# Spectral layer and GeGLU block on one core: the place of the filter sums, of the last n1 transform and of the fourth turn

## The chip, the cores and the metric

The kernel runs on one core of one Trainium2 chip. The core has a matrix engine (TensorE, in the profile PE for its matmuls and PEld for its weight loads), a vector engine (VectorE, DVE), a scalar engine (ScalarE, ACT), a general engine (GpSimd, POOL) and a queue engine (SyncE, SP), each with an instruction stream of its own. They are ordered among one another by semaphores only. Matmuls write to PSUM, which has eight banks; everything else lies in SBUF. The metric is the device time in microseconds (us). Before the change it is 502.81 us, the median of 8 runs (502.54 to 502.91).

## The reference

The input x has 2048 tokens of 576 values in bfloat16. Two sublayers are computed, each behind a layer norm:

```python
def _A_ref(x, w_r, w_i):
    B, S, D = x.shape
    X = rfft2(x.astype(float32), axes=(-2, -1))
    X = X * (w_r + 1j * w_i)
    return irfft2(X, s=(S, D), axes=(-2, -1)).astype(bfloat16)

def _B_ref(x, w_gate, w_up, w_down):
    return (gelu(x @ w_gate) * (x @ w_up)) @ w_down

h  = x + _A_ref(layernorm(x), w_r, w_i)
h2 = h + _B_ref(layernorm(h), w_gate, w_up, w_down)
```

The filter w_r + i w_i has 2048 x 289 values, w_gate and w_up are 576 x 4608, w_down is 4608 x 576.

## The kernel before

The kernel is written as one list of operations in program order. Each operation names its engine, the data it reads and the data it writes. From this list the kernel derives the waits: an operation waits for those before it, on any engine, whose data it needs or whose buffer it takes over. On PE the program order alone is relied on; on DVE, ACT and POOL a dependence inside the same engine is a wait as well. Each engine works off its own operations in the order of the list, so where an operation stands in the list settles what it queues behind.

Tokens are numbered s = 16 n1 + n2, with n1 on the 128 partitions; there are 16 token tiles, one for each n2.

**Layer norm and first transform** (to about 20 us). The statistics of the tiles are taken in five groups. Each group's reciprocal deviation scales the table of the n1 transform (ATS, line 472 on DVE for the first two groups and the last, line 467 on POOL for the third and fourth), and matmuls with x as weights give U, which DVE and ACT copy out of PSUM.

**Spectral stage** (about 20 to 53 us). The frequencies form 16 groups, worked through in the order 1 to 15, 0; in what follows group i is the i-th in this order. Each group goes through these steps:

- `st_D`: six matmuls (line 600), the transform over the 576 values, even and odd halves in two banks; ACT copies the even half (line 603).
- `st_U`: DVE adds the halves (A, line 610) and subtracts them (S, line 613).
- `st_B`: six matmuls (line 626), the rest of the n1 transform; ACT copies the result (YS, line 629).
- `st_T`: DVE multiplies by the filter in two products (T0, T1, line 635). One of them uses a negated copy of w_i, which POOL writes for each group (line 674).
- `st_Z`: DVE sums the two products (Z, line 640).
- `st_V`: six matmuls (line 654), the first part of the inverse n1 transform; ACT copies the result into V (line 665), for the last group DVE and ACT do so in three parts (lines 660 and 662).

One loop (line 676) runs these in a software pipeline: turn i issues `st_D` and `st_U` of group i, `st_B` and `st_T` of group i - 2, and `st_V` of group i - 4. The sum `st_Z` of group i - 3 is issued by `st_U` of group i, between its add and its subtract. The last groups differ: the sum of group 13 follows directly on its products, the last group's products and sums are cut into columns 0 to 127 and the rest, and the sum of group 14 stands behind the first of these products.

POOL's 16 negations wait for the halves of w_i that they use and for the last scaled table of the first transform, `("ATS", NT - 1)`, written by DVE. The loads of the filter are issued on SP's queue. On POOL's queue stand, behind the negations, the loads of the gate weights: those of the first two blocks directly, those of the last two where the filter's buffer comes free, after the last product.

**Inverse stage** (about 53 to 77 us). For each of the 16 tiles c, `st_I(c)` runs six matmuls (line 723), the inverse transform over the values, into two banks given by `islot`; ACT copies them into GS (line 732). `st_N(c)` runs four matmuls (line 762), the last part of the inverse n1 transform, into banks 4 to 7, and DVE adds the result to x (line 765). In program order `st_N(c - 1)` follows `st_I(c)`. The first block of four tiles is normalised on the way (`norm`, DVE and POOL) and turned by `turn_pe`: five matmuls with the unit matrix (line 807) into two banks of the pair used by `st_I`, which ACT copies into HT0 (line 809). `TURN` gives the steps after which the four turns are issued, 8, 10, 12 and 14; `islot` skips a bank pair behind each.

**Gate, up and down** (from about 75 us). Four blocks of 512 tokens. `gu` issues the gate and up matmuls (line 861), two at a time on 64 rows each, with a lag of six matmuls between the halves: `gu(0)` issues the first six of the first half alone. Behind them, still in `gu(0)`, stands `st_N` of the last tile, 15. ACT applies the gelu (line 873), DVE multiplies (line 874). Then the down matmuls (line 884) follow with the final add and the store.

```python
for i in range(NG + 4):
    if i < NG:
        st_D(i); st_U(i)
    ...
    if 2 <= i < NG + 2:
        st_B(i - 2)
    if 2 <= i <= NG:
        st_T(i - 2, 0); st_T(i - 2, 1)
    ...
    if i >= 4:
        st_V(i - 4)
```

Of the kernel before, what the change touches and what calls it, by code (L numbers as in the profile page):

```python
# [7 lines left out]
ALU = mybir.AluOpType  # L8

S, D, K2 = 2048, 576, 289  # L10
KW = 290
# [284 lines left out]
def _build(nc, A_x, A_w_r, A_w_i, B_w_gate, B_w_up, B_w_down, out):  # L296
# [76 lines left out]
    def banks(b, n, w):  # L373
        return PS[:, b * 512:(b + n) * 512].rearrange("p (a c) -> p a c", a=n)[:, :, 0:w]
# [215 lines left out]
    def dbank(i):  # L590
        return 6 if i == 2 else 2 * ((i if i < 2 else i - 3) % 2)

    def st_D(i):
# [7 lines left out]
                                                                        start=(dt == 0), stop=(dt == 2)),  # L601
                     r=uk[us] + ["FT"], w=[("PS", b)])
        P.op(ACT, lambda a, sl=sl, b0=b0: a.activation(ES[:, sl, :], bank(b0, 0, 128, 0, 2 * HK), ACTF.Copy), r=[("PS", b0)], w=[("E", sl)])


    def st_U(i):
        sl, b0, s3 = i % 2, dbank(i), i % 3
        e2 = ES[:, sl, :].rearrange("p (a b) -> p a b", a=2)
        o2 = bank(b0 + 1, 0, 128, 0, 2 * HK).rearrange("p (a b) -> p a b", a=2)
        P.op(DVE, lambda v, e2=e2, o2=o2, s3=s3: v.tensor_tensor(CUS[:, s3, :, 0:HK], e2, o2, op=ALU.add), r=[("E", sl), ("PS", b0 + 1)], w=[("CU", s3)])  # L610
        if i >= 3:
            st_Z(i - 3)
        P.op(DVE, lambda v, e2=e2, o2=o2, s3=s3: v.tensor_tensor(CUS[:, s3, :, K2 - 1:HK - 1:-1], e2[:, :, 0:HK - 1], o2[:, :, 0:HK - 1], op=ALU.subtract),  # L613
             r=[("E", sl), ("PS", b0 + 1)], w=[("SU", s3)])

# [14 lines left out]


    def st_T(i, t_, q0=0, q1=KW, hs=(0, 1)):
        g, sl = GORD[i], i % 2
        w_ = (slice(1, None, -1), slice(2, 0, -1))[t_]
        P.op(DVE, lambda v: v.tensor_tensor(TP[:, sl, t_, :, q0:q1], YS[:, sl, :, q0:q1], WS[:, g, w_, q0:q1], op=ALU.mult),  # L635
             r=[("Y", sl), ("Wn", i), "Yz", "Zz"] + wkeys[0 if 1 <= g < 9 else 1], w=[("T", sl, t_, h) for h in hs])

    def st_Z(i, q0=0, q1=KW, hs=(0, 1)):
        sl, z3 = i % 2, i % 3
        P.op(DVE, lambda v: v.tensor_tensor(ZS[:, z3, :, q0:q1], TP[:, sl, :, 0, q0:q1], TP[:, sl, :, 1, q0:q1], op=ALU.add),  # L640
             r=[("T", sl, t_, h) for t_ in range(2) for h in hs], w=[("Z", z3, h) for h in hs])


    VBANKS = {NG - 4: (0, 0, 1), NG - 2: (2, 2, 3), LAST: (0, 1, 4)}
# [27 lines left out]
    P.alias(["J0", "J1", "ZD"] + [(n_, c) for n_ in ("ATB", "ATS") for c in range(NT)], ["Vfree"])  # L672
    for i in range(NG):
        P.op(POOL, lambda v, g=GORD[i]: v.tensor_scalar(WS[:, g, 0, :], WS[:, g, 2, :], -1.0, None, op0=ALU.mult),  # L674
             r=[k for k in wkeys[0 if 1 <= GORD[i] < 9 else 1] if k[2] == 1] + ["Wz", ("ATS", NT - 1)], w=[("Wn", i)])
    for i in range(NG + 4):
        if i < NG:
            st_D(i)
            st_U(i)
        if i == NG:  # L680
            st_Z(NG - 3)
        if 2 <= i < NG + 2:
            st_B(i - 2)
        if 2 <= i <= NG:
            st_T(i - 2, 0)
            st_T(i - 2, 1)
        if i == NG + 1:
            st_T(LAST, 0, 0, 128, (0,))
            st_Z(LAST - 1)
            st_T(LAST, 1, 0, 128, (0,))  # L690
            st_T(LAST, 0, 128, KW, (1,))
            st_Z(LAST, 0, 128, (0,))
            st_T(LAST, 1, 128, KW, (1,))
            st_Z(LAST, 128, KW, (1,))
        if i == NG + 3:
            idle_ft(3, 5)
        if i >= 4:
            st_V(i - 4)
# [14 lines left out]
    vkeys = vk[0] + vk[1] + vk[2]  # L713


    TURN = (8, 10, 12, 14)

    def islot(c):
        return (c + sum(c > t for t in TURN)) % 2
# [36 lines left out]
    def st_N(c):  # L756
        sl = c % 2
        for h in range(2):
            b = 4 + 2 * sl + h
            for i in range(2):  # L760
                rhs = GS[:, sl, i, 288:0:-1] if h else GS[:, sl, i, 0:288]
                P.op(PE, lambda t, b=b, h=h, i=i, c=c, rhs=rhs: t.matmul(bank(b, 0, 128, 0, 288), IT[:, h * i, c, :], rhs, start=(i == 0), stop=(i == 1)),  # L762
                     r=[("G", sl, i), "IT"], w=[("PS", b)])
# [37 lines left out]
    def turn_pe(c):  # L801
        hs = c % 4
        t0, t1 = 128 * c, 128 * c + 128
        b0 = 2 * ((TURN[c] + 1 + c) % 2)
        for k in range(5):
            b, o = b0 + k // 4, 128 * (k % 4)
            P.op(PE, lambda t, b=b, o=o, k=k, hs=hs: t.matmul(bank(b, 0, 128, o, o + 128), HN[:, hs, 128 * k:128 * k + 128], IDT[:, :], start=True, stop=True),  # L807
                 r=[("HN", hs, 0), ("HN", hs, 1), "IDT"], w=[("PS", b)])
        P.op(ACT, lambda a, t0=t0, t1=t1, b0=b0: a.activation(HT0[:, 0:5, t0:t1], PS[:, b0 * 512:b0 * 512 + 640].rearrange("p (k e) -> p k e", k=5), ACTF.Copy),
             r=[("PS", b0), ("PS", b0 + 1)], w=[("HT", 0, c, 0)])  # L810

    st_I01()
    for c in range(1, NT):
        if c >= 2:
            st_I(c)
        st_N(c - 1)
        if 2 <= c < 6:
            square(c - 2, OS[:, c % 2, :], ("OS", c % 2, 0))
        if c == 5:
            ln2_a(0)  # L820
        if c == 6:
            ln2_b(0)
            ln2_c(0)
            norm(0, DVE)
            norm(1, POOL)
        if c == 7:
            norm(2, DVE)
            norm(3, POOL)
        if c in TURN:
            turn_pe(TURN.index(c))  # L830

    P.alias(ukeys + [(n_, a) for n_ in ("CU", "SU") for a in range(3)], [("WD", j) for j in range(9)])
    for j in range(9):
# [14 lines left out]
    def gu(n):  # L848
        for s_ in range(9 * (n - 1) + LAG, 9 * n + LAG):
            for half in range(2):  # L850
                m, j = divmod(s_ - LAG * half, 9)
                if not 0 <= m < 144:
                    continue
                tb, f = m // 36, m % 36
                o, wt = (ASEQ, BSEQ)[half][j]
                kt = 4 if wt == 8 else wt % 4
                h0 = 64 * half
                HT = HTS[tb % 2]
                b = 2 * (m % 3) + o
                aft = [half_done[m, o]] if half and (j == 0 or j == 4) else []  # L860
                op = P.op(PE, lambda t, h0=h0, kt=kt, wt=wt, f=f, b=b, HT=HT, s=(half == 0 and j in (0, 5)), e=(half == 1 and j in (3, 8)): t.matmul(  # L861
                    bank(b), WGU[h0:h0 + 64, f // 9, wt, 128 * (f % 9):128 * (f % 9) + 128], HT[h0:h0 + 64, kt, :], start=s, stop=e),
                    r=[("HT", tb % 2, i, k) for i in range(4) for k in range(5)] + [("WG", f // 9, i) for i in range(4)],
                    w=[("PS", b)], after=aft)
# [80 lines left out]
```

## Time and profile before

| | |
|---|---|
| median of 8 runs | 502.81 us (502.54 to 502.91) |
| the profiled execution's own time | 502.74 us |
| its span, first to last instruction | 500.9 us |
| mean granted TensorE clock | 0.997 |
| PE busy (matmuls) | 492.6 us, 98% of the span |
| DVE busy | 182.4 us, 36% |
| ACT busy | 158.4 us, 32% |
| POOL busy | 39.8 us, 8% |
| gate/up matmuls on the chain that ended last | 56% of the span |
| down matmuls on that chain | 28% |
| DVE on that chain | 7% |

The profile is one execution. The span leaves out what lies around the first and last instruction, 1.84 us here. "Busy" is the time in which an engine works on instructions, overlapping ones counted once; PE's matmuls are pipelined and their ends are modelled. The chain of waits goes back from the last instruction to whatever released it, and so on to the start. In rows of the timeline the first number is the start in us, the second the length in us of the instruction or, with x2 and the like, of several merged ones; the tiles stand as output <- inputs. "L640" is line 640 of the kernel.

### The profile page before, as it was taken

The numbers are of one execution on the slowest core, as the hardware profiler recorded it, in microseconds if no ns is written. First come the engines' busy times: TensorE is split into PE (matmuls) and PEld (weight loads), VectorE is DVE, ScalarE is ACT, GpSimd is POOL, SyncE is SP. The second block draws the span as 40 slices with busy tenths as digits, with TensorE's granted clock in tenths as the row PEclk, the third lists the DMA queues.
The fourth block names the chain that finished last, engine by engine and source line by source line (L and its number), as shares of the span: only waits on it lengthen the run. The fifth ranks groups of instructions, "written<-read, shape, count | busy, mean of one in ns | idle before, by whom it ended". The sixth has DMA issues, their size and how long they took to land.

```text
span 500.9 us, 9971 instructions
## 1 busy us (share of the span) xinstructions
PE 492.6 (98%) x4318; PEld 298.8 (60%) x4319; DVE 182.4 (36%) x391; ACT 158.4 (32%) x296; POOL 39.8 (8%) x49
## 2 busy tenths in 40 slices
PE   7999999999999999999999999999999999999998
PEld 2787774444457764444477744444677544444775
DVE  6899663344421114433311034433201233333111
ACT  7888776653220012323300023232100123233000
POOL 3654290000000000000000000000000000000000
PEclk9899999999999999999999999999999999999999
DMA  8769998001100000100000001100000000000000
GB/s 284 166 202 313 326 295 313 2 7 25 26 1 19 18 13 20 22 14 1 2 13 12 19 18 22 23 1 1 1 18 19 13 1 1 1 3 1 12 19 19
DMA packets 25948, 28.64 MB, mean 57 GB/s; under 512 B 11568, under 2 KB 19888, under 8 KB 25776
## 3 DMA queue, kind: packets, MB, share of 16 engines
q1 hardware_dynamic: 23328, 17.39, 12.2%
q0 software_dynamic: 2576, 10.62, 6.4%
q8 instruction: 34, 0.56, 0.5%
q14 instruction: 10, 0.08, 0.1%
HBM read 23.66 MB, written 2.36 MB: 52 GB/s over the span
## 4 chain that ended last, share of the span: by engine, by line
PE 90%; DVE 7%; issue 1%; DMA 1%; ACT 1%; DVEq 0%
PE PS L861 56%; PE PS L884 28%; PE PS L723 3%; DVE TP L635 2%; PE PS L762 2%; DVE ST L440 1%; DVE ZS L640 1%; DVE CUS L613 1%; DMA XO<-in_A_x_dram 1%; PE PS L600 1%; DVE U L505 0%; DVE ATS L472 0%; ACT JNK L431 0%; PE PS L807 0%; PE PS L654 0%
## 5 line engine op out<-in xcount | busy, mean ns | idle before, releaser
L861 PE MATMUL PS<-HT,WGU 64*128 64x512 bf16 x2592 | 281.9, 376 | 0.0
L861 PEld LDWEIGHTS PS<-HT,WGU 64*128 64x128 bf16 x2592 | 137.3, 94 | 143.4 <-issue 1.2
L873 ACT ACTIVATE GL<-PS 128x512 bf16<-128x512 f32 x144 | 85.9, 597 | 289.3 <-PE PS L861 289.3
L874 DVE TENSOR_TENSOR AT<-GL,PS 128x512 bf16<-128x512 bf16 x144 | 99.0, 688 | 174.2 <-PE PS L861 172.5
L884 PE MATMUL PS<-WD,AT 128*128 128x288 bf16 (+2 forms) x1152 | 141.8, 286 | 0.0
L884 PEld LDWEIGHTS PS<-WD,AT 128*128 128x128 bf16 x1152 | 111.0, 98 | 31.5 <-issue 1.7
L887 DVE TENSOR_TENSOR OS<-PS,XO 128x288 bf16<-128x288 f32 (+2 forms) x32 | 14.7, 458 | 125.8 <-PE PS L884 125.8
L674 POOL TENSOR_SCALAR WS<-WS 128x290 bf16<-128x290 bf16 x16 | 15.9, 996 | 9.6 <-DMA WS<-in_A_w_i_dram 5.8
L765 DVE SCALAR_TENSOR_TENSOR XO<-PS,XO 128x576 bf16<-128x576 f32 x16 | 12.1, 756 | 8.4 <-PE PS L762 8.4
L600 PE MATMUL PS<-FT,U 128*128 128x290 bf16 x96 | 14.4, 287 | 0.5 <-DVE U L505 0.5
L723 PE MATMUL PS<-DT,V 128*128 128x289 bf16 x96 | 14.6, 287 | 0.2 <-DVE V L660 0.2
L635 DVE TENSOR_TENSOR TP<-YS,WS 128x580 bf16<-128x580 bf16 (+2 forms) x34 | 14.2, 456 | 0.3 <-issue 0.3
L654 PE MATMUL PS<-VT,ZS 128*128 128x256 bf16 x96 | 13.1, 272 | 1.0 <-DVE ZS L640 1.0
L665 ACT ACTIVATE V<-PS 128x768 bf16<-128x768 f32 x15 | 12.2, 811 | 1.2 <-PE PS L654 1.0
L629 ACT ACTIVATE YS<-PS 128x578 bf16<-128x578 f32 x16 | 10.5, 655 | 3.3 <-PE PS L626 3.1
L732 ACT ACTIVATE GS<-PS 128x578 bf16<-128x578 f32 x15 | 9.8, 655 | 4.2 <-PE PS L723 4.1
L723 PEld LDWEIGHTS PS<-DT,V 128*128 128x128 bf16 x96 | 8.9, 97 | 3.5 <-issue 0.4
L600 PEld LDWEIGHTS PS<-FT,U 128*128 128x128 bf16 x96 | 9.2, 98 | 3.0 <-issue 0.6
L753 ACT ACTIVATE OS<-XO 128x576 bf16<-128x576 bf16 x16 | 10.8, 675 | 0.0
L626 PE MATMUL PS<-CUS,BT 128*128 128x289 bf16 (+2 forms) x96 | 10.7, 246 | 0.0
L762 PE MATMUL PS<-GS,IT 128*128 128x288 bf16 x64 | 10.5, 285 | 0.0
L654 PEld LDWEIGHTS PS<-VT,ZS 128*128 128x128 bf16 x96 | 8.5, 97 | 3.0 <-DVE ZS L640 1.2
(58 smaller groups left out, 156.6 us busy)
## 6 DMA issues: line engine op xcount, KB each, us to landing
WD<-in_B_w_down_dram POOLq DMA_DIRECT2D x9, 576.0 KB, 8.6
WGU<-in_B_w_up_dram SPq DMA_DIRECT2D x4, 1152.0 KB, 9.7
WGU<-in_B_w_gate_dram POOLq DMA_DIRECT2D x4, 1152.0 KB, 10.9
out_dram<-OS SPq DMA_DIRECT2D x30, 72.0 KB, 1.6
XO<-in_A_x_dram SPq DMA_DIRECT2D x3, 576.0 KB, 6.9
IT<-c_itab SPq DMA_DIRECT2D x1, 1024.0 KB, 7.9
HT<-HN SPq DMA_TRANSPOSE x60, 2.4
XO<-in_A_x_dram SPq DMA_DIRECT2D x2, 288.0 KB, 3.0
```

What stands on the lines that cost most here:

```text
L600: P.op(PE, lambda t, b=b, o=o, dt=dt, us=us, g=g: t.matmul(bank(b, 0, 128, 0, 2 * HK), U[:, us, g, :, :], FT[:, o, dt, :], start=(dt == 0) ...
L635: P.op(DVE, lambda v: v.tensor_tensor(TP[:, sl, t_, :, q0:q1], YS[:, sl, :, q0:q1], WS[:, g, w_, q0:q1], op=ALU.mult), r=[("Y", sl), ("Wn" ...
L654: P.op(PE, lambda t, b=b, o=o, c=c, zp=zp, sl=sl, sp_=sp_: t.matmul(bank(b, 0, 128, o, o + 256), ZS[:, sl, zp, 128 * c:128 * c + 128], VT[ ...
L665: P.op(ACT, lambda a, g=g, src=src: a.activation(V[:, :, :, g, :], src, ACTF.Copy), r=[("PS", bs[0]), ("PS", bs[2]), "Vfree"], w=[("V", g, ...
L674: P.op(POOL, lambda v, g=GORD[i]: v.tensor_scalar(WS[:, g, 0, :], WS[:, g, 2, :], -1.0, None, op0=ALU.mult), r=[k for k in wkeys[0 if 1 <= ...
L723: P.op(PE, lambda t, b=b, h=h, i=i, kt=kt, c=c: t.matmul(bank(b, 0, 128, 0, K2), V[:, kt, c, :, :], DT[:, 3 * h + i, 0:K2], start=(i == 0) ...
L762: P.op(PE, lambda t, b=b, h=h, i=i, c=c, rhs=rhs: t.matmul(bank(b, 0, 128, 0, 288), IT[:, h * i, c, :], rhs, start=(i == 0), stop=(i == 1) ...
L861: op = P.op(PE, lambda t, h0=h0, kt=kt, wt=wt, f=f, b=b, HT=HT, s=(half == 0 and j in (0, 5)), e=(half == 1 and j in (3, 8)): t.matmul(ban ...
L873: P.op(ACT, lambda a, s2=s2, b0=b0: a.activation(GL[:, s2, :], bank(b0), ACTF.Gelu_apprx_tanh), r=[("PS", b0)], w=[("GL", s2)])
L874: P.op(DVE, lambda v, s2=s2, b0=b0, f=f: v.tensor_tensor(AT[:, f, :], GL[:, s2, :], bank(b0 + 1), op=ALU.mult), r=[("GL", s2), ("PS", b0 + ...
L884: P.op(PE, lambda t, b=b, d0=d0, d1=d1, f=f, p=p: t.matmul(bank(b, 0, 128, 0, d1 - d0), AT[:, f, 128 * p:128 * p + 128], WD[:, f, d0:d1], ...
L887: P.op(DVE, lambda v, b=b, d0=d0, d1=d1, p=p, c=c: v.tensor_tensor(OS[:, p % 2, d0:d1], bank(b, 0, 128, 0, d1 - d0), XO[:, c, d0:d1], op=A ...
```

## The change

In the spectral loop the functions `st_U`, `st_T` and `st_Z` are dissolved. The add and subtract of a group now follow its `st_D`, and both products and the sum follow its `st_B`, so that the sum of group i - 2 stands directly behind its two products in turn i of the loop. The last group is still cut into two column ranges; each range now runs its two products and its sum in a row, and the sum of group 14 stands behind its own products. POOL's negations no longer wait for the last scaled table.

In the inverse stage the fourth turn moves from behind `st_N(13)` to behind `st_I(15)`, ahead of `st_N(14)`, and DVE copies it out of PSUM instead of ACT. `st_N(15)` moves out of `gu(0)` to directly behind `st_N(14)`, so that it stands ahead of the six first gate/up matmuls. With 15 in place of 14 in `TURN`, tile 15 uses the bank pair 0, 1 and the fourth turn the pair 2, 3, the other way round than before.

```diff
         P.op(ACT, ... a.activation(ES[:, sl, :], ...), r=[("PS", b0)], w=[("E", sl)])
-
-    def st_U(i):
-        sl, b0, s3 = i % 2, dbank(i), i % 3
         P.op(DVE, ... v.tensor_tensor(CUS[:, s3, :, 0:HK], e2, o2, op=ALU.add), ...)
-        if i >= 3:
-            st_Z(i - 3)
         P.op(DVE, ... v.tensor_tensor(CUS[:, s3, :, K2 - 1:HK - 1:-1], ..., op=ALU.subtract), ...)
...
         P.op(ACT, ... a.activation(YS[:, sl, :, 0:K2], banks(b0, 2, K2), ACTF.Copy), ...)
-    def st_T(i, t_, q0=0, q1=KW, hs=(0, 1)):
-        ...
-    def st_Z(i, q0=0, q1=KW, hs=(0, 1)):
-        ...
+        wk = wkeys[0 if 1 <= g < 9 else 1] + [("Wn", i), "Yz", "Zz"]
+        z3 = i % 3
+        for q0, q1, hs in ((0, 128, (0,)), (128, KW, (1,))) if i == LAST else ((0, KW, (0, 1)),):
+            for t_, w_ in enumerate((slice(1, None, -1), slice(2, 0, -1))):
+                P.op(DVE, ... v.tensor_tensor(TP[:, sl, t_, :, q0:q1], YS[...], WS[...], op=ALU.mult), ...)
+            P.op(DVE, ... v.tensor_tensor(ZS[:, z3, :, q0:q1], TP[:, sl, :, 0, q0:q1], TP[:, sl, :, 1, q0:q1], op=ALU.add), ...)
...
         P.op(POOL, ... v.tensor_scalar(WS[:, g, 0, :], WS[:, g, 2, :], -1.0, None, op0=ALU.mult),
-             r=[...] + ["Wz", ("ATS", NT - 1)], w=[("Wn", i)])
+             r=[...] + ["Wz"], w=[("Wn", i)])
     for i in range(NG + 4):
         if i < NG:
             st_D(i)
-            st_U(i)
-        if i == NG:
-            st_Z(NG - 3)
         if 2 <= i < NG + 2:
             st_B(i - 2)
-        if 2 <= i <= NG:
-            st_T(i - 2, 0)
-            st_T(i - 2, 1)
-        if i == NG + 1:
-            st_T(LAST, 0, 0, 128, (0,))
-            st_Z(LAST - 1)
-            st_T(LAST, 1, 0, 128, (0,))
-            st_T(LAST, 0, 128, KW, (1,))
-            st_Z(LAST, 0, 128, (0,))
-            st_T(LAST, 1, 128, KW, (1,))
-            st_Z(LAST, 128, KW, (1,))
...
-    TURN = (8, 10, 12, 14)
+    TURN = (8, 10, 12, 15)
...
+        src = PS[:, b0 * 512:b0 * 512 + 640].rearrange("p (k e) -> p k e", k=5)
+        if c == 3:
+            P.op(DVE, ... v.tensor_copy(HT0[:, 0:5, t0:t1], src), ...)
+        else:
+            P.op(ACT, ... a.activation(HT0[:, 0:5, t0:t1], src, ACTF.Copy), ...)
...
             st_I(c)
+        if c == NT - 1:
+            turn_pe(3)
         st_N(c - 1)
...
-        if c in TURN:
+        if c in TURN[0:3]:
             turn_pe(TURN.index(c))
+    st_N(NT - 1)
...
     if m < 0:
-        st_N(NT - 1)
         P.alias(fdead, fnew)
         return
```

More of the change, by code (lines that the diff above doesn't have):

```diff
@@ L629, in st_B @@
         P.op(ACT, lambda a, sl=sl, b0=b0: a.activation(YS[:, sl, :, 0:K2], banks(b0, 2, K2), ACTF.Copy), r=[("PS", b0), ("PS", b0 + 1)], w=[("Y", sl)])
-    def st_T(i, t_, q0=0, q1=KW, hs=(0, 1)):
[L633 to L636, printed above, removed]
-    def st_Z(i, q0=0, q1=KW, hs=(0, 1)):
-        sl, z3 = i % 2, i % 3
-        P.op(DVE, lambda v: v.tensor_tensor(ZS[:, z3, :, q0:q1], TP[:, sl, :, 0, q0:q1], TP[:, sl, :, 1, q0:q1], op=ALU.add),
-             r=[("T", sl, t_, h) for t_ in range(2) for h in hs], w=[("Z", z3, h) for h in hs])
+        wk = wkeys[0 if 1 <= g < 9 else 1] + [("Wn", i), "Yz", "Zz"]
+        z3 = i % 3
+        for q0, q1, hs in ((0, 128, (0,)), (128, KW, (1,))) if i == LAST else ((0, KW, (0, 1)),):
+            for t_, w_ in enumerate((slice(1, None, -1), slice(2, 0, -1))):
+                P.op(DVE, lambda v, sl=sl, g=g, q0=q0, q1=q1, t_=t_, w_=w_: v.tensor_tensor(TP[:, sl, t_, :, q0:q1], YS[:, sl, :, q0:q1], WS[:, g, w_, q0:q1], op=ALU.mult),
+                     r=[("Y", sl)] + wk, w=[("T", sl, t_, h) for h in hs])
+            P.op(DVE, lambda v, sl=sl, z3=z3, q0=q0, q1=q1: v.tensor_tensor(ZS[:, z3, :, q0:q1], TP[:, sl, :, 0, q0:q1], TP[:, sl, :, 1, q0:q1], op=ALU.add),
+                 r=[("T", sl, t_, h) for t_ in range(2) for h in hs], w=[("Z", z3, h) for h in hs])
     VBANKS = {NG - 4: (0, 0, 1), NG - 2: (2, 2, 3), LAST: (0, 1, 4)}
@@ L674, in _build @@
         P.op(POOL, lambda v, g=GORD[i]: v.tensor_scalar(WS[:, g, 0, :], WS[:, g, 2, :], -1.0, None, op0=ALU.mult),
-             r=[k for k in wkeys[0 if 1 <= GORD[i] < 9 else 1] if k[2] == 1] + ["Wz", ("ATS", NT - 1)], w=[("Wn", i)])
+             r=[k for k in wkeys[0 if 1 <= GORD[i] < 9 else 1] if k[2] == 1] + ["Wz"], w=[("Wn", i)])
     for i in range(NG + 4):
@@ L808, in turn_pe @@
                  r=[("HN", hs, 0), ("HN", hs, 1), "IDT"], w=[("PS", b)])
-        P.op(ACT, lambda a, t0=t0, t1=t1, b0=b0: a.activation(HT0[:, 0:5, t0:t1], PS[:, b0 * 512:b0 * 512 + 640].rearrange("p (k e) -> p k e", k=5), ACTF.Copy),
-             r=[("PS", b0), ("PS", b0 + 1)], w=[("HT", 0, c, 0)])
+        src = PS[:, b0 * 512:b0 * 512 + 640].rearrange("p (k e) -> p k e", k=5)
+        if c == 3:
+            P.op(DVE, lambda v, t0=t0, t1=t1, src=src: v.tensor_copy(HT0[:, 0:5, t0:t1], src), r=[("PS", b0), ("PS", b0 + 1)], w=[("HT", 0, c, 0)])
+        else:
+            P.op(ACT, lambda a, t0=t0, t1=t1, src=src: a.activation(HT0[:, 0:5, t0:t1], src, ACTF.Copy), r=[("PS", b0), ("PS", b0 + 1)], w=[("HT", 0, c, 0)])
     st_I01()
```

## The prediction

> **What bounds the kernel now.** I read the page first, for the span and the busy shares, then the chain of waits, then the timelines of the three places that the diff touches. From about 53 us on PE runs matmuls end to end; the spectral stage, from about 20 to 53 us, is another matter.
>
> ```profile
> span 500.9 us, 9971 instructions
> ...
> PE 492.6 (98%) x4318; PEld 298.8 (60%) x4319; DVE 182.4 (36%) x391; ACT 158.4 (32%) x296; POOL 39.8 (8%) x49
> ...
> 24.00:50.00 26.00, 25.44 (x237) 21.00 (x236) 25.97 (x69) 22.76 (x40) 13.24 (x15) 1.00 0.84 249
> ```
>
> The last row is the table by stage: 26.00 us, then PE, PEld, DVE, ACT, POOL busy. DVE is busy for 25.97 of 26.00 us, PE for 25.44. The chain of waits agrees (start, length, what); nearly every link from 23.7 to 51.3 us is DVE:
>
> ```profile
> 45.97 0.45 DVE ZS L640
> 46.42 0.07 DVE CUS L613
> 46.49 0.22 issue
> 46.71 0.82 DVE TP L635 x2
> 47.53 0.07 DVE CUS L610
> 47.60 0.21 issue
> 47.81 0.45 DVE ZS L640
> ```
>
> So a microsecond added to DVE's order here is a microsecond of the kernel. What that order costs is in DVE's timeline:
>
> ```profile
> 47.81 0.45 DVE L640 TENSOR_TENSOR ZS<-TP 128x580 bf16<-128x580 bf16 x1
> 48.19 0.45 DVE L613 TENSOR_TENSOR CUS<-ES,PS 128x288 bf16<-128x288 f32 x1
> 48.55 0.82 DVE L635 TENSOR_TENSOR TP<-YS,WS 128x580 bf16<-128x580 bf16 x2
> 49.41 0.46 DVE L640 TENSOR_TENSOR ZS<-TP 128x580 bf16<-128x580 bf16 x1
> ...
> 51.80 0.32 DVE L635 TENSOR_TENSOR TP<-YS,WS 128x324 bf16<-128x324 bf16 x1
> 52.16 0.33 DVE L640 TENSOR_TENSOR ZS<-TP 128x324 bf16<-128x324 bf16 x1
> ```
>
> Instructions last 0.45 us, but one that needs nothing of the one before it starts 0.37 us after it (47.81 to 48.19 to 48.55). The pair at 48.55 lasts 0.82, so its second product started at 48.92 and ended at 49.37. The sum that needs it started at 49.41: 0.49 us after the product, not 0.37. The sum at 52.16 likewise started 0.04 after the end of its product (51.80 + 0.32). A sum right behind its own products costs 0.12 us more than one with another instruction between.
>
> **The order of the filter sums.** Call the DVE work of a group A, S (add and subtract, lines 610, 613), T0, T1 (products, 635), Z (sum, 640). Before, DVE runs T0 T1 A Z S: the next group's A stands between T1 and Z. After, it runs T0 T1 Z A S. Nothing is added or removed; A and Z change places, and each Z waits out its T1. In the trace the full cycle without disturbance is 5 x 0.37 = 1.85 us (44.13 to 45.97 is 1.84). After, 4 x 0.37 + 0.49 = 1.97. Z(0) to Z(12) are so shielded before, Z(13) is not: 13 x 0.12 = 1.56 us.
>
> Is it hidden? PE's cycle is 1.91 us (35.80, 37.72, 39.64 for its first matmuls of a group), below 1.97, so PE becomes the one that waits: behind the PSUM bank that S frees, and as the next matmuls of that group are wanted by DVE some 2 us later (A at 47.45 against its matmuls at 45.52), DVE doesn't starve. ACT is busy for 22.76 of 26.00. I find no cover.
>
> The tail. Before, from Z(13) at 49.41 to the start of the last Z at 52.16 are 2.75 us. After, by the steps of these same rows: T0 0.37, T1 0.37, Z(14) 0.49, first half of the last group T0 0.37, T1 0.21, Z 0.32 (0.29 duration and the wait), second half T0 0.20, T1 0.24, Z 0.36, together 2.93: plus 0.18. Given back behind it: the last matmuls on the filtered data start before at 52.34, after the V matmuls of the group ahead and three idle ones; after, that group's Z is 0.33 us earlier against the last Z, so the first evacuation by DVE (52.76) moves up, and the second, which now queues behind it at 53.10, starts when its own matmul is done, about 52.97. The second inverse matmul (53.57, bank shared with that evacuation) follows: minus 0.13.
>
> **Collisions of DVE and POOL.** POOL's negations (line 674, 16 of 0.94 us) meet T and Z:
>
> ```profile
> 25.45 0.94 POOL L674 TENSOR_SCALAR WS<-WS 128x290 bf16<-128x290 bf16 x1
> ...
> 25.59 0.97 DVE L635 TENSOR_TENSOR TP<-YS,WS 128x580 bf16<-128x580 bf16 x2
> ```
>
> The pair takes 0.97, not 0.82: the first product ended at 26.19, 0.74 after POOL's start. Four more were so held (32.38, 33.59, 37.13, 39.13: by 0.10, 0.23, 0.15, 0.20); with this one 0.83 us in all. The diff puts T, T, Z side by side and moves the phase. I cannot read the new phase from the old trace, so I take the same 0.83, between none (minus 0.83) and a hold of 0.17 for each of the 16 (2.72, plus 1.89); as phases drift rather than lock, I stay at plus 0.
>
> **The earlier negations.** Line 675 loses its wait on the last scaled table. POOL has been idle since 15.49, so the first now waits for the weights alone: the last load of them is issued at 11.22 and lands 6.1 us later, near 17.3, against a start at 18.12 now. It then meets the three scalings of line 472 that start from 17.37 to 17.70, on the path: four U copies follow without a gap (17.87, 2.48 us for four) and the first spectral matmul waits for the third. From below nothing, if DVE gets through first; from above 0.43, by the one row where DVE and POOL run such instructions together: normalisation at 62.80, where two take 1.07 us, the second 0.72 against a least of 0.29. The holds above end 0.29 (0.74 less 0.45) behind POOL's start, so that from a start near 17.4 the scaling of 17.54 would be held to about 17.67; I take 0.15. POOL issues no DMA between these and the second batch, which waits for its own landing at 32.19; the gate loads behind that batch (40.96) stay put, and those behind the last product (52.42) move with it and are wanted some 50 us later (18 gate/up groups of 1.95).
>
> The Trainium skill, SBUF — State Buffer, "Who interferes with whom", says that whichever of the two starts first holds the shared port pair for its whole instruction. By that rule the product at 25.59 would have waited until 26.39; it ended at 26.19, so the trace shows a shorter hold. By the rule a scaling could lose up to 0.94 us, and the sum below would be 505.1.
>
> **The end of the inverse stage.** PE's rows of before:
>
> ```profile
> 72.44 0.66 PE L762 MATMUL PS<-GS,IT 128*128 128x288 bf16 x4
> 72.93 0.44 PE L807 MATMUL PS<-IDT,HN 128*128 128x128 bf16 x5
> 73.35 0.92 PE L723 MATMUL PS<-DT,V 128*128 128x289 bf16 x6
> 74.11 0.65 PE L762 MATMUL PS<-GS,IT 128*128 128x288 bf16 x4
> 74.70 1.47 PE L861 MATMUL PS<-HT,WGU 64*128 64x512 bf16 x6
> 76.09 0.67 PE L762 MATMUL PS<-GS,IT 128*128 128x288 bf16 x4
> ```
>
> From 72.93 to the next gate/up matmul at 76.69 are 3.76 us. The same matmuls in the new order, by start-to-start steps: tile 15's d transform 0.76, turn 0.42, n1 transform of tile 14 0.49 (72.44 to 72.93), of tile 15 0.59 (the step at 74.11, into the 64-row matmuls), six gate/up matmuls at 0.216 (70.05 us for 648 is 0.108, two at a time) 1.30: 3.56. One change of matmul shape and back is saved: minus 0.20. Two waits have to hold. Tile 15's transform needs ACT's evacuation, which starts 0.96 after the d matmuls (73.35 to 74.31) and lasts 0.66: ready at 1.62, wanted at 1.67. The gate/up matmuls need the turned tile: DVE starts 0.48 after the turn (72.93 to 73.41 on ACT), at 1.24, is free by then (the add of tile 13 ends near 0.96), and lasts about 0.81, an estimate from its copies of 512 columns (0.68) and 256 (0.42); ready near 2.1, wanted at 2.26. What queues behind that copy on DVE are the adds of tiles 14 and 15, whose banks are wanted two gate/up groups later. If a wait fails, up to 0.3 is lost instead. ACT loses 0.70 us of work and loads its table earlier; nothing waits for that.
>
> **Sum.** 1.56 + 0.18 - 0.13 + 0 + 0.15 - 0.20 = 1.56. The profiled execution took 502.74 (0.07 below the median of 502.81): 502.74 + 1.56 = 504.30.
>
> The Trainium skill, VectorE: DVE Perf Modes, "The DRAIN you can't avoid", says that a semaphore between chained DVE instructions costs nothing extra, since each waits for the pipeline anyway. It speaks against this sum; rows 49.41 and 52.16 disagree with it. By it the sum would be 502.56.
>
> **Rivals.** Slower by over 0.2% (1.01 us, about what a measurement can tell from no change) begins at 503.82.
>
> First, not slower: the wait between T1 and Z costs little in the steady cycle, because it overlaps with what DVE would have done anyway. Without the 1.74 us of waits the sum is 502.56. For it: DVE is a pipelined engine and only the tail shows the wait, in three rows; against it: those rows agree to a hundredth. It decides below 0.085 us a sum (1.74 less the 0.48 between 504.30 and 503.82, over fifteen).
>
> Second, the new phase lets POOL's instructions miss DVE's: 504.30 - 0.83 = 503.47, within 0.2%. For it, POOL's first batch moves 0.7 us ahead; against it, the second batch, which holds 0.68 of the 0.83, starts where it did.
>
> Third, they collide more: T, T, Z in a row are a larger target, up to 504.30 + 1.89 = 506.19; with half of that, 505.2. The head's 0.43 adds 0.28.
>
> Fourth, PE was the true bound and has slack to give. Then only 1.97 less 1.91 a cycle counts, 13 x 0.06 = 0.78: 503.5. Against it: DVE's 0.03 us of idle time in 26.
>
> **How the numbers follow.** Forecast as summed, 503.82 to 505.0: 0.60. Collisions worse, above that: 0.15. Fewer collisions: 0.10. PE's slack: 0.06. Waits free: 0.06. Waits free and collisions gone (501.7): 0.03. Slower 0.75, same 0.22, faster 0.03. The range leaves out 0.1 on each side: 503.2 to 505.3.
>
> **What would show it.** Right: DVE's cycle near 1.97 us with Z starting 0.04 after T1 ends; PE idle within the stage; the first spectral matmul up to 0.3 later than 19.89; the first gate/up matmul after the last n1 transform, about 0.5 us behind the old place beyond the stage's shift, but its successors 0.2 ahead. Wrong: Z starting 0.37 after T1, or DVE idle in the stage, or more than six products longer than 0.5 us.

## The result, and the profile after

The changed kernel takes 504.58 us, the median of 11 runs (503.87 to 506.01), against 502.81 us (502.52 to 503.48, 31 runs) for the kernel before: a ratio of 1.0037 with a 95% interval of 1.003 to 1.0045. It is slower by 1.77 us. The profiled execution took 504.58 us, 1.84 more than that of before (502.74).

The page of the kernel after: the span, the busy times, and the chain that ended last by engine.

```profile
span 502.7 us, 9973 instructions
...
PE 493.4 (98%) x4318; PEld 298.6 (59%) x4319; DVE 184.7 (37%) x392; ACT 158.2 (31%) x295; POOL 39.9 (8%) x49
...
PE 93%; DVE 5%; issue 1%; DMA 1%; ACT 1%; DVEq 0%
```

PE's and DVE's busy times hardly moved, and DVE's share of the chain even fell. None of this shows where the time went; the spectral stage does. The table by stage of the kernel after (start and end, length, busy time of PE, PEld, DVE, ACT and POOL, clock, DMA share, GB/s) has for the spectral stage

```profile
24.00:50.00 26.00, 24.89 (x225) 19.89 (x224) 25.55 (x64) 22.16 (x38) 13.11 (x15) 1.00 0.83 256
```

In the same 26 us PE ran 225 matmuls where it ran 237, and DVE 64 instructions where it ran 69. DVE is now idle for 0.45 us; these are thirteen pauses of 0.035 us, each in front of a sum. DVE's timeline of the kernel after shows it (start, length, what):

```profile
43.00 0.46 DVE L629 TENSOR_TENSOR TP<-YS,WS 128x580 bf16<-128x580 bf16 x1
43.50 0.46 DVE L631 TENSOR_TENSOR ZS<-TP 128x580 bf16<-128x580 bf16 x1
43.87 0.45 DVE L606 TENSOR_TENSOR CUS<-ES,PS 128x290 bf16<-128x290 f32 x1
44.24 0.45 DVE L607 TENSOR_TENSOR CUS<-ES,PS 128x288 bf16<-128x288 f32 x1
44.60 0.83 DVE L629 TENSOR_TENSOR TP<-YS,WS 128x580 bf16<-128x580 bf16 x2
45.47 0.46 DVE L631 TENSOR_TENSOR ZS<-TP 128x580 bf16<-128x580 bf16 x1
45.84 0.46 DVE L606 TENSOR_TENSOR CUS<-ES,PS 128x290 bf16<-128x290 f32 x1
```

The second product starts at 43.00 and ends at 43.46; the sum that needs it starts at 43.50, half a microsecond behind the product's start, whereas the add behind the sum follows after 0.37 (43.87). From add to add is 1.97 us (43.87 to 45.84); it was 1.84. At the same place the chain of waits of the kernel after has the products, a short wait of 0.02 and the sum, which the next link leaves behind after 0.04:

```profile
42.72 0.75 DVE TP L629 x2
43.47 0.02 issue
43.50 0.04 DVE ZS L631
43.53 0.12 issue
...
43.87 0.45 DVE CUS L606
```

PE now waits for the sum in every cycle. Its timeline of the kernel after has the matmuls of `st_B` and behind them those of `st_V`:

```profile
45.51 0.67 PE L620 MATMUL PS<-CUS,BT 128*128 128x289 bf16 x6
46.08 0.82 PE L645 MATMUL PS<-VT,ZS 128*128 128x256 bf16 x6
```

The second row starts 0.15 us behind the end of the sum (45.47 + 0.46), as in all thirteen cycles, and 0.57 behind the first row; where PE does not wait, this step is 0.51. The modelled ends cover such a short wait (the first row's 0.67 reaches past 46.08). So the chain of waits, which runs through PE's matmuls from 22 to 41.5 us, does not show that PE bounds the stage there, and in the list of waits stand only the longer ones in the tail, from 49.4 us on (in total, times, longest; before, 1.0 us in 3 times):

```profile
PE PS L645 <- DVE ZS L631: 1.6, 4, 0.6
```

A second effect is on top. This is the timeline of all engines of the kernel after around 34 us:

```profile
33.85 1.05 DVE L629 TENSOR_TENSOR TP<-YS,WS 128x580 bf16<-128x580 bf16 x2
34.09 1.02 POOL L665 TENSOR_SCALAR WS<-WS 128x290 bf16<-128x290 bf16 x1
...
34.94 0.46 DVE L631 TENSOR_TENSOR ZS<-TP 128x580 bf16<-128x580 bf16 x1
35.19 1.01 POOL L665 TENSOR_SCALAR WS<-WS 128x290 bf16<-128x290 bf16 x1
```

The two products take 1.05 us where they take 0.83 undisturbed: the second one is held for 0.23 us by the negation that started 0.24 behind the first. The same happens to the pairs that start at 36.05, 38.24 and 40.44, and once early, in the pair that starts at 23.77: five holds of 0.23, 1.14 us together, against 0.83 before.

The tail of the stage, DVE's timeline of the kernel after:

```profile
51.38 0.46 DVE L631 TENSOR_TENSOR ZS<-TP 128x580 bf16<-128x580 bf16 x1
51.76 0.82 DVE L629 TENSOR_TENSOR TP<-YS,WS 128x580 bf16<-128x580 bf16 x2
52.62 0.46 DVE L631 TENSOR_TENSOR ZS<-TP 128x580 bf16<-128x580 bf16 x1
...
54.32 0.33 DVE L631 TENSOR_TENSOR ZS<-TP 128x324 bf16<-128x324 bf16 x1
```

From the sum of group 13 to the last sum are 2.94 us, where there were 2.75. And PE's timeline at the end of the inverse stage, where the time came back:

```profile
74.48 0.66 PE L739 MATMUL PS<-GS,IT 128*128 128x288 bf16 x4
74.98 0.91 PE L700 MATMUL PS<-DT,V 128*128 128x289 bf16 x6
75.73 0.44 PE L784 MATMUL PS<-IDT,HN 128*128 128x128 bf16 x5
76.00 1.30 PE L739 MATMUL PS<-GS,IT 128*128 128x288 bf16 x8
77.24 2.13 PE L844 MATMUL PS<-HT,WGU 64*128 64x512 bf16 x12
```

The last d transform, the fourth turn, eight n1 matmuls in one piece, and then gate/up matmuls without a gap. From 74.98 to the second six of the gate/up matmuls (78.54, which is 77.24 and six steps of 0.216) are 3.56 us; before, 3.76.

### The profile page after: what moved, and what is told of

The parts are those of the page before. It is cut to its first block, busy times and chain, and to the rows that moved or that the text cites. A ratio compares the mean times of both kernels' runs of the same rounds, so it can differ in the third digit from the quotient of the medians.

```text
span 502.7 us, 9973 instructions
## 1 busy us (share of the span) xinstructions
PE 493.4 (98%) x4318; PEld 298.6 (59%) x4319; DVE 184.7 (37%) x392; ACT 158.2 (31%) x295; POOL 39.9 (8%) x49
## 4 chain that ended last, share of the span: by engine, by line
PE 93%; DVE 5%; issue 1%; DMA 1%; ACT 1%; DVEq 0%
PE PS L844 56%; PE PS L866 28%; PE PS L700 2%; PE PS L600 2%; PE PS L739 2%; PE PS L645 1%; DVE ST L440 1%; DVE TP L629 1%; PE PS L620 1%; DMA XO<-in_A_x_dram 1%; DVE U L505 0%; DVE CUS L606 0%; DVE CUS L607 0%; DVE ATS L472 0%; ACT JNK L431 0%
```

## The experiments

Theory: on DVE, a sum that stands right behind its own products costs 0.12 us more than a shielded one, DVE bounds the stage, and thirteen sums and the tail are the loss; the rest of the change gives 0.2 back. Rivals: the loss comes from the negations on POOL, which collide more or start earlier; the new end of the inverse stage costs something; or the wait between product and sum is free in the steady cycle.

### The three parts one by one

The kernel before with the new order of the sums alone:

```diff
-        if i >= 3:
-            st_Z(i - 3)
...
-        if i == NG:
-            st_Z(NG - 3)
...
             st_T(i - 2, 1)
+            st_Z(i - 2)
         if i == NG + 1:
             st_T(LAST, 0, 0, 128, (0,))
-            st_Z(LAST - 1)
             st_T(LAST, 1, 0, 128, (0,))
-            st_T(LAST, 0, 128, KW, (1,))
             st_Z(LAST, 0, 128, (0,))
+            st_T(LAST, 0, 128, KW, (1,))
```

> The kernel before with one part of the change alone: each sum directly behind its two products, POOL's wait and the end of the inverse stage as before. Theory (each sum waits out its product, 0.12 us, on the engine that bounds the stage): 13 x 0.13 + 0.19 in the tail - 0.12 given back behind it = 1.76 us slower, and up to 0.3 more where POOL's negations lock onto the products; 504.3 to 505.0, and DVE's cycle 1.97 us without POOL. Rival (the loss comes from POOL's earlier negations, not from the order of the sums): within 0.3 us of 502.81. Rival (PE bounds the stage): 13 x 0.06 = 0.8 slower, 503.6.

Measured: 504.64 us (504.17 to 504.86, 5 runs) against 502.77 (26 runs), ratio 1.0032 [1.0019, 1.0044]. This part alone loses 1.87 us, all of what the whole change loses. Its products are held like those of the kernel after; from DVE's timeline of this kernel:

```profile
34.08 1.05 DVE L633 TENSOR_TENSOR TP<-YS,WS 128x580 bf16<-128x580 bf16 x2
35.17 0.46 DVE L638 TENSOR_TENSOR ZS<-TP 128x580 bf16<-128x580 bf16 x1
...
36.28 1.05 DVE L633 TENSOR_TENSOR TP<-YS,WS 128x580 bf16<-128x580 bf16 x2
37.36 0.46 DVE L638 TENSOR_TENSOR ZS<-TP 128x580 bf16<-128x580 bf16 x1
```

The kernel before with the new end of the inverse stage alone:

```diff
-    TURN = (8, 10, 12, 14)
+    TURN = (8, 10, 12, 15)
...
+        if c == 3:
+            P.op(DVE, ... v.tensor_copy(HT0[:, 0:5, t0:t1], src), ...)
...
             st_I(c)
+        if c == NT - 1:
+            turn_pe(3)
...
+    st_N(NT - 1)
...
-            st_N(NT - 1)
```

> The kernel before with the other part alone: the fourth turn behind the d matmuls of tile 15 and copied by DVE, the last n1 transform ahead of the first gate/up matmuls. Theory: one change of matmul shape and back is saved and both waits hold, 0.20 us faster, 502.6. Rival (the gate/up matmuls wait for DVE's copy of the turned tile): no change or up to 0.3 slower, 502.8 to 503.1, with PE idle ahead of the first gate/up matmul.

Measured: 502.58 us (502.41 to 503.03, 11 runs), ratio 0.9994 [0.9985, 1.0003]. Run again beside the last experiments but one:

> The new end of the inverse stage alone, once more, beside the paced kernel on the same chip. Theory: 0.20 us faster than the kernel before, 502.5 to 502.6.

Measured: 502.46 us (502.38 to 503.01, 11 runs) against 502.68, ratio 0.9996 [0.9988, 1.0005]. The 0.2 us lie inside the interval of both measurements; in the traces they are plain. From the second matmul of the inverse stage to the second six gate/up matmuls 22.92 us pass in every kernel with the new end, and 23.12 in every one with the old.

The kernel before with the negations' wait on the last scaled table taken out, and nothing else:

```diff
-             r=[...] + ["Wz", ("ATS", NT - 1)], w=[("Wn", i)])
+             r=[...] + ["Wz"], w=[("Wn", i)])
```

> The kernel before with POOL's wait on the last scaled table taken out of what the negations need, nothing else. Theory: the weights land about when the scalings run, so that POOL starts 0.2 to 0.8 us earlier; a collision with a scaling costs 0.03 to 0.15 at the head, and the first batch's phase against the products shifts: within 0.3 us of 502.81, with more spread from run to run than the 0.96 us of before. Rival (the earlier start is the main loss of the change): 504 or more.

Measured: 502.98 us (502.83 to 503.41, 11 runs), ratio 1.0002 [0.9993, 1.0011]: no difference that can be told. The first negation started at 17.75 us, the landing of its weights, against 18.12 before.

The other way round, the kernel after with the old order of the sums put back and the other two parts kept:

```diff
         P.op(DVE, ... op=ALU.add), ...)
+        if i >= 3:
+            st_Z(i - 3)
         P.op(DVE, ... op=ALU.subtract), ...)
...
+        if 2 <= i <= NG:
+            st_T(i - 2, 0)
+            st_T(i - 2, 1)
```

> The changed kernel with one part undone: each sum again behind the next group's add, the last group as before; POOL's earlier negations and the new end of the inverse stage stay. Theory: the order of the sums carries the whole loss, so that this lands on the sum of the two other parts, 502.8 (0.2 lost at POOL, 0.2 won at the end). Rival (the parts work together): 503.5 or more.

Measured: 502.44 us (502.12 to 502.76, 11 runs) against 502.68, ratio 0.9994 [0.9985, 1.0003]. With the order put back the loss is gone; the 0.2 us that this expectation put down to the earlier negations are not seen either. That the new end causes the loss falls, and so does the earlier start of the negations as its cause.

### How much of it is POOL's

The order of the sums could lose by the waits of DVE or by the collisions with POOL. Without the negations there is nothing to collide with:

```diff
-            for t_, w_ in enumerate((slice(1, None, -1), slice(2, 0, -1))):
+            for t_, w_ in enumerate((slice(1, 3), slice(2, 0, -1))):
...
-    for i in range(NG):
-        P.op(POOL, ... v.tensor_scalar(WS[:, g, 0, :], WS[:, g, 2, :], -1.0, None, op0=ALU.mult), ...)
```

> The changed kernel with POOL's negations left out (the first product takes w_i as it is, so the output has the wrong sign in one term). Theory: the collisions, five holds of 0.23 us in the trace after, go, and nothing else: 504.58 - 1.14 = 503.4, and the spread of 2.1 us from run to run shrinks to some 0.5, since it comes from the phase of POOL's batches against DVE's cycle. Rival (the waits behind the products are what varies): the spread stays. Rival (collisions cost nothing on the path): 504.5.

Measured: 504.15 us (503.67 to 505.26, 10 runs) against 502.77, ratio 1.0028 [1.0019, 1.0037]. The expected 503.4 is missed. No product was held, but the first of them came late. DVE's timeline of this kernel has

```profile
23.17 0.45 DVE L607 TENSOR_TENSOR CUS<-ES,PS 128x288 bf16<-128x288 f32 x1
...
24.48 0.83 DVE L629 TENSOR_TENSOR TP<-YS,WS 128x580 bf16<-128x580 bf16 x2 [0.86 <-DMA WS<-in_A_w_r_dram]
```

DVE waited 0.86 us for the filter. The negations had also kept the gate loads behind them on POOL's queue. Without them 2.6 MB of gate weights set off at once, and the first half of w_r landed at 24.5 us, where it lands at 19.9 in the kernel after. The experiment had removed two things at once. Again with the first gate load held back until the add of group 12:

```diff
-            P.dma(eng, WGU[...], src[...], f"wgu{o}{j}", w=[("WG", j, o)])
+            P.op(eng, ... e.dma_start(WGU[...], src[...]), w=[("WG", j, o)], dma=f"wgu{o}{j}",
+                 after=(adds[12],) if (j, o) == (0, 0) else ())
```

> As the run without negations of the changed kernel (one term keeps the wrong sign), but the first gate load on POOL's queue now waits for the add of group 12, about when the negations would have let it go; without them it had started at once and delayed the filter's loads. Theory: the filter lands before 20 us again, the first product starts near 23.8, the five holds of 0.23 us stay away: 504.58 - 1.14 = 503.4, and the runs lie within 0.6 us of one another. Rival (run-to-run spread has nothing to do with POOL): spread near 2 us as in the changed kernel.

Measured: 503.51 us (503.31 to 503.74, 11 runs) against 502.69 (502.45 to 503.44, 31 runs), ratio 1.0016 [1.0007, 1.0025]. From DVE's timeline of this kernel, at the place of the holds:

```profile
33.80 0.82 DVE L631 TENSOR_TENSOR TP<-YS,WS 128x580 bf16<-128x580 bf16 x2
34.66 0.46 DVE L633 TENSOR_TENSOR ZS<-TP 128x580 bf16<-128x580 bf16 x1
35.03 0.45 DVE L608 TENSOR_TENSOR CUS<-ES,PS 128x290 bf16<-128x290 f32 x1
```

No hold, the sum still 0.04 behind its product, the cycle 1.97. The spread of the runs fell from 2.1 us to 0.4. The same edit on the kernel before:

> The kernel before without POOL's negations, its first gate load held back in the same way (one term keeps the wrong sign). Theory: the five holds of the trace before, 0.83 us, go: 502.0; PE's cycle of 1.91 us then bounds DVE's of 1.84 so that up to half of it may not show, 502.0 to 502.4. The difference to the changed kernel without negations is then the order of the sums and the end of the inverse stage alone: 13 x 0.13 + 0.19 - 0.12 - 0.20 = 1.5 us. Rival (the waits behind the products cost nothing by themselves): less than 0.3 us between the two.

Measured: 502.14 us (502.04 to 502.36, 11 runs), ratio 0.9989 [0.998, 0.9997]. So without POOL in the stage the whole change still costs 503.51 - 502.14 = 1.37 us. The waits of the sums are not free, and the rival that they are falls. With POOL the two kernels are 1.77 apart, so some 0.4 of the loss needs POOL.

The 1.37 is below the 1.5 expected, and the trace of the kernel before without negations shows why. With the holds gone, DVE catches up with the engines that feed it. The chain of waits of this kernel runs through PE's matmuls, 1.91 us a group without a gap, up to 46.7 us, then through copies of ACT, and DVE waits for the last of them (DVE's timeline of this kernel):

```profile
50.05 0.29 DVE L637 TENSOR_TENSOR TP<-YS,WS 128x256 bf16<-128x256 bf16 x1 [0.21 <-ACT YS L631]
```

Its tail, from the sum of group 13 to the last, is 2.99 us instead of 2.75. So 0.24 of the 0.83 us of holds came back as a wait, and the 0.4 is not the price of the collisions alone.

### When POOL starts

If a hold depends on where in DVE's cycle a negation starts, tying each negation to that cycle should remove the holds and keep the negations. In the kernel after, the negation for group i + 1 of the second batch waits for the sum of group i - 2:

```diff
-    for i in range(NG):
+    def neg(i, after=()):
...
+    for i in range(8):
+        neg(i)
     for i in range(NG + 4):
...
+            if 7 <= i < NG - 1:
+                neg(i + 1, (zs[i - 2],))
```

> The changed kernel with POOL's second batch paced: the negation for group i + 1 starts when the sum of group i - 2 is done, so that its reads fall beside the add and the subtract, which read PSUM. Theory (the second batch locks onto DVE's cycle, two negations of 1.10 us to a cycle of 2.20): the four holds of 0.23 us go, 504.58 - 0.91 = 503.7, no product after 32 us longer than 0.5 us. Rival (the holds come from the number of negations, wherever they stand): 504.5.

Measured: 504.01 us (503.84 to 504.66, 9 runs), ratio 1.0025 [1.0015, 1.0034]. No product after 32 us is longer than 0.46 us; the holds are gone as expected. The time misses 503.7 by 0.3. And on the kernel before, with its order of the sums and the new end, each of these negations waiting for the add of group i:

```diff
+            if 7 <= i < NG - 1:
+                neg(i + 1, (adds[i],))
```

> The kernel before, its order of sums kept, with the new end of the inverse stage and with POOL's second batch paced: the negation for group i + 1 waits for the add of group i, so that it comes in behind the sum that is running and reads beside the subtract. Theory: the 0.68 us of holds of the second batch go, and 0.20 at the end: 502.81 - 0.88 = 501.9, less what PE's cycle of 1.91 us keeps (DVE's alone is 1.84): 501.9 to 502.3. Rival (a negation that starts ahead of the subtract is late enough to hold the next product): no better than the end alone, 502.6.

Measured: 502.44 us (502.26 to 502.8, 11 runs), ratio 0.9994 [0.9985, 1.0003], against an expected 501.9 to 502.3. Once more, beside the new end alone:

> The paced kernel with the old order of sums and the new end, once more. In its trace the stage from the first spectral matmul to the first gate/up matmul took 54.78 us against 55.19 with the new end alone, so 0.4 us faster than that one, 502.1 to 502.2; rival (the pacing gives back at the start what it wins): equal within 0.15.

Measured: 502.42 us (502.26 to 502.55, 11 runs), ratio 0.9994 [0.9985, 1.0003]: no better than the new end alone (502.46). In the trace of that one the negations of the second batch cost 0.75 us of holds; they are gone here, and the tail is 0.19 longer (2.93), as in the kernel before without negations. So the last add of the kernel came 0.56 us earlier. The last row of DVE's timeline with the new end alone, then in this kernel:

```profile
498.43 0.29 DVE L892 TENSOR_TENSOR OS<-PS,XO 128x128 bf16<-128x128 f32 x1 [1.36 <-PE PS L889]
```

```profile
497.87 0.29 DVE L899 TENSOR_TENSOR OS<-PS,XO 128x128 bf16<-128x128 f32 x1 [1.35 <-PE PS L896]
```

This gain reached the end of the work and was lost behind it. In the trace's semaphore records, POOL's last two steps at the close of the program stand 0.42 us apart in this kernel and 0.08 with the new end alone. The three traces with paced negations hold 69 records of POOL where that of the new end alone holds 62, and each of the three has one more instruction load in the last 60 us. From the DMA view of that stretch (packets, MB, share), this kernel:

```profile
q14 instruction: 3, 0.02, 0.1%
```

and the new end alone:

```profile
q14 instruction: 2, 0.02, 0.1%
```

Seven of the eight paced negations wait for two engines, their own and DVE, and the second wait is an instruction by itself: seven more. The wait on the own engine is not needed for the data, since a negation reads and writes nothing of the negation ahead:

```diff
+        if i >= 9:
+            op.deps = {d for d in op.deps if d[0].eng != POOL}
```

> The kernel before with the new end and the paced negations, as in the run before it, but the seven paced negations no longer also wait for the negation ahead of them on their own engine (nothing of it is needed). That takes seven waiting instructions out of POOL's code. What is open: the paced kernel ended its last add 0.56 us earlier than the one with the new end alone (497.87 against 498.43) and its last store landed as much earlier, yet its span was only 0.2 shorter and its median the same. In its trace POOL's last two steps at the close stand 0.42 us apart and a third small instruction load lies in the last 60 us; with the new end alone they stand 0.07 apart and there are two such loads. Theory: the seven extra instructions carry POOL's code over a boundary, and the close waits 0.35 us for the load. Then here the two steps are 0.07 apart again, there are two loads, and the median is 502.42 less 0.35, 502.07 (501.9 to 502.25). Rival: the gain is lost elsewhere (the close itself, the store); the span stays 500.5 and the median 502.3 to 502.5. Rival: the wait on the own engine had a part in the pacing; then products are held again after 32 us and the last add comes later than 497.9.

Measured: 502.06 us (501.94 to 502.78, 11 runs) against 502.63 (502.45 to 503.5, 15 runs), ratio 0.9988 [0.9979, 0.9997]. POOL's two steps are 0.08 apart, the DMA view has two such loads again:

```profile
q14 instruction: 2, 0.02, 0.1%
```

and the last add starts where it did (497.90). The 0.35 us came back: 502.42 to 502.06, of which 0.05 lies in the kernel before too (502.68 and 502.63 beside them), and all runs but one are below all of the other's. That the loads are what the close had waited for is the reading; the runs show that the instructions, the third load and the 0.35 us come and go together. The paced kernel after, whose close also had the 0.42, would by the same 0.35 have been at 503.66, its expectation; that was not run. The timeline of this last kernel shows the place that a negation now has in the cycle:

```profile
36.09 0.45 DVE L642 TENSOR_TENSOR ZS<-TP 128x580 bf16<-128x580 bf16 x1
36.25 1.08 POOL L676 TENSOR_SCALAR WS<-WS 128x290 bf16<-128x290 bf16 x1 [0.76 <-DVE CUS L612]
36.46 0.44 DVE L615 TENSOR_TENSOR CUS<-ES,PS 128x288 bf16<-128x288 f32 x1
...
36.82 0.82 DVE L637 TENSOR_TENSOR TP<-YS,WS 128x580 bf16<-128x580 bf16 x2
```

It starts 0.16 behind the start of a sum, runs 1.08 us instead of 0.94, and the products take their undisturbed 0.82. Of the versions that keep the negations, this is the one that is below the kernel before by more than its interval: 0.57 us, and 2.5 below the changed one.

## Why the prediction was right

It said 504.30 us, 503.2 to 505.3, slower; measured were 504.58. By its steps, in the profiled executions:

| step | predicted | in the trace |
|---|---|---|
| order of the sums, thirteen cycles | +1.56 | +1.63 |
| tail to the last sum | +0.18 | +0.19 |
| given back behind the tail | -0.13 | -0.12 |
| collisions with POOL | 0 | +0.31 |
| earlier negations at the head | +0.15 | +0.04 |
| end of the inverse stage | -0.20 | -0.20 |
| sum | +1.56 | +1.85 |

The rows in the trace are worked out thus. From the first product to the last sum are 30.55 us after and 28.42 before, 2.13 more; less the holds (1.14 - 0.83) and the tail (2.94 - 2.75), 1.63 are left for the thirteen sums, 0.125 each; the cycles of 1.97 and 1.84 say 0.13. From the last sum to the second matmul of the inverse stage are 1.30 us, 1.42 before. The first spectral matmul starts at 19.93, 19.89 before. The 1.85 agree with the 1.84 between the two executions. That the forecast is off by no more than 0.29 is in part luck: 0.11 too much at the head made up for a part of the 0.31 that it lacked at the collisions.

**The order of the sums** was right in its size and in where it shows: DVE's cycle of 1.97 and the sum 0.04 behind its product, with no cover: the rival by which only 1.97 less PE's 1.91 a cycle would count (503.5) falls with the 1.63. Removing the negations on both sides leaves most of the loss standing (1.37 us), and putting the order back removes it. One sign that the prediction named as speaking against it, DVE idle in the stage, did occur: the 0.45 us of idle time are the pauses between product and sum themselves. The rest of the 0.12 us is not idle at all: it is the overlap that a dependent instruction cannot have. That is why the share of busy time barely moved.

The Trainium skill, VectorE: DVE Perf Modes, "The DRAIN you can't avoid", holds, by a measurement on eight copies in a row, that a semaphore between chained DVE instructions costs nothing extra there, and adds that a next instruction that is not held starts earlier. The rows here agree with the second part and not with the first: two independent instructions of 0.45 us start 0.37 apart, a dependent one starts 0.49 behind, and the order of the sums, with the same products, sums and waits, costs 1.87 us.

**The collisions** are the term that was mis-sized. The prediction took the old 0.83 us unchanged, on the ground that "phases drift rather than lock". They locked. Undisturbed, DVE's cycle of 1.97 is shorter than two negations back to back, 2 x 1.10 = 2.19 (34.09 to 36.28 in POOL's timeline). A hold of 0.23 stretches the cycle to 2.20, so that the second next negation starts at the same place in it, and holds again: four cycles in a row, until POOL ran out of negations. The old order is not safe from this. In the trace of the kernel before the holds lie apart and differ in size (0.10 to 0.23), but in that of the new end alone (its second measurement), which has the old order, they lock too. Its POOL timeline, then its DVE timeline:

```profile
33.96 6.06 POOL L674 TENSOR_SCALAR WS<-WS 128x290 bf16<-128x290 bf16 x6
```

```profile
35.07 1.02 DVE L635 TENSOR_TENSOR TP<-YS,WS 128x580 bf16<-128x580 bf16 x2
...
37.12 1.02 DVE L635 TENSOR_TENSOR TP<-YS,WS 128x580 bf16<-128x580 bf16 x2
...
39.17 1.02 DVE L635 TENSOR_TENSOR TP<-YS,WS 128x580 bf16<-128x580 bf16 x2
```

Here a negation follows the last after 1.02 us, and a hold of 0.20 stretches the cycle of 1.84 to 2.05, again two negations. The holds of that execution are some 0.9 us together. How often each order locks is not known, so the 0.31 of the table is the difference of two executions and no fixed price of the new order. The four runs that tied the negations to the cycle, on both orders of the sums, had no hold after 32 us, so where a negation starts decides it.

The Trainium skill, SBUF — State Buffer, "Who interferes with whom", lets whichever engine comes first keep the shared port for its whole instruction. The runs show shorter holds: a product that met a running negation of 1.02 us (34.09) was late by 0.23 and ended at 34.90, 0.21 before it, and in the last kernel above the negation that started during a sum, at 36.25, and ran to 37.33 did not hold the products at 36.82.

**The head** came out smaller because its premise failed: the weights of the first negations landed at 17.8 us in this execution, not near 17.3, and the three scalings had already started (17.41, three in 0.58). The collision there was not seen, so its price stays open; taking the wait out alone changed the time by no more than could be told. The 0.04 is no price either: in the traces of these runs the first spectral matmul starts anywhere from 19.86 to 20.23, with the wait and without.

**The end of the inverse stage** and **the tail** were right to 0.01 us. In the rows of before a step between matmuls of 128 and of 64 rows is longer by 0.10 than one without a change (0.59 against 0.49) or by 0.09 (1.39 against 1.30), and the new order has one of each less. The turn's copy by DVE, estimated at 0.81 us, took 0.82, started at 76.20, and the gate/up matmuls did not wait for it.

What stays open: why the runs of the changed kernel spread over 2.1 us, and those of the kernel before over 1.0. Without the negations, and with the gate loads held back, the spread was 0.4; without the negations alone it stayed at 1.6. The time at which the filter's loads land, which settles when POOL starts, would explain both, but single executions without a profile don't show it.

## What to carry to other kernels

On an engine whose instructions overlap, the distance between a producer and its consumer in the same engine's order is worth counting: put one independent instruction between them, and price a change of order by start-to-start steps, not by busy time. Where two engines disturb each other and the period of one is close to a multiple of the other's, work out whether one disturbance brings the other back to the same place; if it can, tie the off-path engine to a fixed place of the bounding one's cycle. When an experiment takes work away, ask what that work had been holding back, and when a gain is seen at the last instruction and not in the time, look at the close of the program.

## What the runs showed of the hardware that was not expected

- Collisions of DVE and POOL can lock: four holds of 0.23 us in a row at 2.20 us a cycle, and, on the old order, three of 0.20 in a row at 2.05.
- A negation of 0.94 us that starts 0.16 us after a sum has begun takes 1.08 us itself and holds neither that sum nor the products behind it.
- 16 small instructions on POOL were also a brake on DMA: without them the gate loads that stand behind them set off earlier and the first half of w_r landed 4.6 us later (24.5 against 19.9 us).
- Seven more waiting instructions on POOL cost 0.35 us at the close of the program, where a third instruction load appeared in the last 60 us; taking them out gave both back.
- One change of matmul shape (from 128 rows to 64 and back) less was worth 0.20 us, the same in every trace.
